# Scans that take their identity from a PSUM bank, and sums of weights spread over three units

## The chip, the cores and the metric

The kernel runs on one core of a Trainium2 chip. The metric is the device time of one execution in microseconds (us), and the median over several executions is compared. The engines are named as in the profile: PE is TensorE, with PEld for its weight loads, DVE is VectorE, ACT is ScalarE, POOL is GpSimd and SP is SyncE, which issues most DMAs.

## The reference, cut to what matters

A state space layer (Mamba2 SSD) over 4 batches, 8 heads, 768 tokens, head size 32 and state size 16 is followed by a two-layer network with a PReLU (256 to 2048 to 256).

```python
cum = np.cumsum(np.log(np.clip(a, 1e-06, 1.0)), axis=-1)       # per chunk
L = np.exp(cum[:, :, :, None] - cum[:, :, None, :]) * causal
M = np.einsum('bhin,bhjn->bhij', Cc, Bc) * L                   # decays times gram matrix
y = M @ xc + (Cc @ state) * np.exp(cum)                        # and the state is carried on
...
h = x @ w_in                                                   # x: 3072 tokens x 256
g = np.maximum(h, 0.0) + alpha * np.minimum(h, 0.0)
out = g @ w_out
```

All data are float32.

## The kernel before, in words

The tokens are cut into chunks of 128, two chunks make a pair (12 pairs), and two pairs make a group of 512 tokens (6 groups). The five engines run the instructions in the order in which the program writes them, one queue for each engine.

**First stage (to about 103 us).** Group 0 goes through the network plainly: `hidden` (L521 to L525) and `output` (L534), in two passes of 256 tokens, while the weights are still being loaded and converted (`convert_a`, `convert`, with POOL at L201 and L230). In between, `ssm` advances the state space layer of pairs 0 to 3.

**Units.** Groups 1 to 5 go through the network in 20 units, `quad(g, z)`: a unit takes four blocks of 128 hidden features (z = 0 to 3) and all 512 tokens, and forms both matrix products by a scheme with 7 block products instead of 8. That scheme needs sums of weights (`weight_sums`, L562, on POOL: `in_sums` from w_in, `out_sums` from w_out, each in four parts for the first (`q0` = 0) and for the last (`q0` = 4) four feature pairs; part 3 overwrites one block of the weights), and sums of tokens (`token_sums`, L574, POOL). In a unit PE fills two PSUM buffers A and Y in turn (L616), ACT and DVE take them out (L624 to L644, and the PReLU at L599 and L601), and POOL forms differences of the results (L650, L659). PE's second products (`product`, L591, n = 1 to 7) of a unit are issued within the unit after it, at the steps of `places`; they accumulate in the four PSUM banks `bank(0)` to `bank(3)`. The fifth product uses the first half of bank 3, and the second half is not used. `combine` (L676 to L698) takes the banks out once per group, within z = 0 of the group after.

**Scans.** `pair` is a generator: each `ssm` call runs it to its next `yield`. For the matrix of decays `dec`, a DVE scan runs over 8 heads x 128 columns: state = a * state + identity, and a zero at the start of each head's row of `a` starts it anew. For pairs 0 and 1 the first operand lies in PSUM (L371), for 2 and 3 one scan of 1024 columns reads both operands from SBUF (L366). For the later pairs 4 to 11 (`fine`), which belong to groups 2 to 5 and are made during the units of groups 1 to 4, `half_decays` (L376) issues scans of 512 columns with `abc` and `ident_h`, both in SBUF. `steps` places them: in z = 0 after steps 2, 3 and 14 and in z = 1 after step 1 for the first pair, in z = 2 after steps 1, 2, 9 and 14 for the second. After the scans come the gram matrices (PE, L475) and their product with the decays (DVE, L480).

`after(j)` is called between the steps of a unit and issues what is due there: products, sums, `combine`, and a stage of a pair, in that order. An instruction that shares a tile with another, in PSUM the tile's bank, waits for it where the program's dependency tracking says so.

Of the kernel before, what the change touches and what calls it, by code (L numbers as in the profile page):

```python
# [12 lines left out]
ALU = mybir.AluOpType  # L13
# [9 lines left out]
def kernel(  # L23
# [25 lines left out]
    nc = tc.nc  # L49
# [7 lines left out]
    Q = 128  # L57
# [16 lines left out]
    HT = GT // 2  # L74
# [25 lines left out]
    def bank(i):  # L100


        return ps_q.tile([P, 512], F32, name="bank", tag=f"q{i}")
# [104 lines left out]
    def convert(dst, src, sg, add=nc.gpsimd):  # L208
# [14 lines left out]
        else:  # L223
            for i in range(2):
# [10 lines left out]
    ident_h = const.tile([P, H * Q], F32, name="ident_h")  # L235
    nc.vector.tensor_copy(out=ident_h.rearrange("p (h t) -> p h t", h=H),
                          in_=ident.unsqueeze(1).to_broadcast([P, H, Q]))
# [40 lines left out]

    held = {}
    bns = {}  # L280

    def rows_scan(i):

        rows = loads.pop(("r", i))
        d0 = prep.tile([RW, Q + 1], F32, name="r0")
        nc.vector.tensor_scalar(out=d0[:, :Q], in0=rows, scalar1=1e-6, scalar2=1.0,
                                op0=ALU.max, op1=ALU.min)
        nc.vector.memset(d0[:, Q:], 0.0)
        pr = prep.tile([RW, Q], F32, name="pr")
        nc.vector.tensor_tensor_scan(out=pr[:, ::-1], data0=d0[:, 1:][:, ::-1],  # L290
                                     data1=ends[:RW, ::-1], initial=0.0,
                                     op0=ALU.mult, op1=ALU.add)
        held[i] = d0
        return pr
# [60 lines left out]
    def pair(gp):  # L355

        b, c = divmod(2 * gp, CPB)
        nat, abc, xt, ap = loads["p", gp]
        last = c + 2 == CPB
        dec = work.tile([P, 2, H, Q], F32, name="dec")  # L360
        dv = dec.rearrange("p k h t -> p k (h t)")
# [10 lines left out]
                                             initial=0.0, op0=ALU.mult, op1=ALU.add)  # L372

        def half_decays(k, w):
            ws = slice(512 * w, 512 * w + 512)
            nc.vector.tensor_tensor_scan(out=dv[:, k, ws], data0=abc[k][:, ws],  # L376
                                         data1=ident_h[:, ws], initial=0.0, op0=ALU.mult,
                                         op1=ALU.add)

        ahead = {}  # L380
        if not abc:
# [7 lines left out]
        if not abc:  # L389
            pf = work.tile([P, 2 * Q], F32, name="pf")  # L390
            nc.vector.tensor_scalar(out=ap, in0=ap, scalar1=1e-6, scalar2=1.0, op0=ALU.max,
                                    op1=ALU.min)
            for k in range(2):
                ks = slice(k * Q, (k + 1) * Q)
                nc.vector.tensor_tensor_scan(out=pf[:, ks], data0=ap[:, ks], data1=zeros,
                                             initial=1.0, op0=ALU.mult, op1=ALU.add)
# [44 lines left out]
        for k in range(nk):  # L441
            for w in range(KC):
                ws = slice(64 * w, 64 * w + 64)
# [21 lines left out]
        if fine:  # L465
            for w in range(2):
                half_decays(1, w)
                yield


        for k in range(2):
# [6 lines left out]
            for r in range(2):  # L478
                hs = slice(4 * r, 4 * r + 4)
# [7 lines left out]
        for k in range(2):  # L487
            if st[k] is not None:
                for w in range(KC):
                    ws = slice(64 * w, 64 * w + 64)  # L490
# [3 lines left out]
        for k in range(2):  # L494
            for w in range(KC):
                for q in range(4):
                    h = 4 * w + q
# [3 lines left out]
        g, q = divmod(2 * gp, GC)  # L501
        if q == 0:
            xts[g] = xtp.tile([P, KC, GT], F32, name="xT")
        for w in range(KC):
            nc.scalar.copy(out=xts[g][:, w, q * Q : (q + 2) * Q],
                           in_=y[w].rearrange("p k t -> p (k t)"))
# [21 lines left out]
    def output(f, half=None):  # L528

        if f == 0:  # L530
            pos[0] = [bank(i).rearrange("p (t m) -> p t m", t=2) for i in range(GC // 2)]
        gt = gts[0, f]
        for t in range(GC) if half is None else range(2 * half, 2 * half + 2):
            nc.tensor.matmul(pos[0][t // 2][:, t % 2], gt[:, t * Q : (t + 1) * Q], w_out[:, f],  # L534
                             start=(f == 0 and t % 2 == 0), stop=(f == NF - 1),
                             skip_group_check=True)
        if f == NF - 1 and half:
            for i, po in enumerate(pos.pop(0)):
                o_sb = op.tile([P, 2, d_model], F32, name="o_sb")
                nc.scalar.copy(out=o_sb, in_=po)  # L540
                t0 = 2 * i * Q
                nc.sync.dma_start(
                    out=out[t0 : t0 + 2 * Q, :].rearrange("(s p) m -> p s m", p=Q), in_=o_sb)
# [5 lines left out]
    wi = w_in.rearrange("p k (q i m) -> p q i k m", i=2, m=P)  # L549
    out_sums, in_sums = [], []  # L550

    def weight_sums(w, sums, q0, part):


        if not sums:
            sums.extend(wld.tile([P, NQ, P], F32, name=f"ws{i}", tag="raw") for i in range(3))
        qs = slice(q0, q0 + 4)
        a11, a12, a21, a22 = w[:, qs, 0, 0], w[:, qs, 0, 1], w[:, qs, 1, 0], w[:, qs, 1, 1]
        s1, s2, s4 = (t[:, qs] for t in sums)
        o, x0, x1, f = ((s1, a21, a22, ALU.add), (s2, s1, a11, ALU.subtract),  # L560
                        (s4, a12, s2, ALU.subtract), (a21, a11, a21, ALU.subtract))[part]
        nc.gpsimd.tensor_tensor(out=o, in0=x0, in1=x1, op=f)  # L562

    wqt = wq.rearrange("p q j i m -> p q i j m")
    xsums = {}

    def token_sums(g):

        b11, b12 = (xts[g][:, 0, h * HT : (h + 1) * HT] for h in range(2))
        b21, b22 = (xts[g][:, 1, h * HT : (h + 1) * HT] for h in range(2))  # L570
        t = xsp.tile([P, 4, HT], F32, name="xs")
        t1, t2, t3, t4 = (t[:, i] for i in range(4))
        for o, x0, x1 in ((t1, b12, b11), (t2, b22, t1), (t3, b22, b12), (t4, b21, t2)):
            nc.gpsimd.tensor_tensor(out=o, in0=x0, in1=x1, op=ALU.subtract)  # L574
        xsums[g] = t1, t2, t3, t4

    ms = {}
# [3 lines left out]
    def product(g, z, n):  # L581

        if z == 0 and n == 1:
            ms[g] = [bank(i).rearrange("p (h t) -> p h t", h=2) for i in range(4)]
        i, h = HALVES[n]
        s1, s2, s4 = out_sums
        for p in range(2):
            q = 2 * z + p
            w = {1: wq[:, q, 0, 0], 2: wq[:, q, 1, 0], 3: s4[:, q], 4: wq[:, q, 1, 1],
                 5: s1[:, q], 6: s2[:, q], 7: wq[:, q, 0, 1]}[n]  # L590
            nc.tensor.matmul(ms[g][i][:, h], w, blocks[g, z][n][:, p],  # L591
                             start=(q == 0 and h == 0), stop=(q == NQ - 1),
                             skip_group_check=True)
# [119 lines left out]
    def finish(g, i):  # L713
        turn(g, i, ends_of[g][i], slice(0, GT), [nc.sync])
# [3 lines left out]
    def ssm(gp, stages=1):  # L718

        if gp not in pairs:  # L720
            pairs[gp] = pair(gp)
        for i in range(stages):
            next(pairs[gp], None)
# [5 lines left out]
    for i in range(3, 6):  # L729
# [9 lines left out]
    first = {1: (1, 1), 4: (1, 1), 6: (1, 1), 8: (1, 1), 10: (1, 1), 12: (1, 1), 14: (2, 1)}  # L739
    second = {0: (2, 1), 1: (2, 1), 2: (2, 1), 3: (2, 1), 5: (2, 1), 6: (3, 1), 7: (3, 1),  # L740
              8: (3, 1), 9: (3, 1), 11: (3, 1), 13: (3, 1)}
    in_steps = {6: ((0, 0), (0, 1)), 8: ((0, 2), (4, 0)), 10: ((4, 1), (4, 2)), 12: ((0, 3),)}
    for n in range(2):
        for f in range(NF):
            i = (n * NF + f) // 2
# [16 lines left out]
            if n and f in in_steps:  # L762
# [2 lines left out]
    early[0] = None  # L765
    token_sums(1)

    steps = {(0, 1): 0, (0, 2): 0, (0, 3): 0, (0, 9): 0, (0, 14): 0,
# [3 lines left out]

    places = {3: 1, 5: 2, 8: 3, 9: 5, 11: 7, 13: 6, 14: 4}
    for i in range(NZ * (NG - 1)):
        g, z = divmod(NZ + i, NZ)
        nxt = 2 * g + 2

        def after(j, g=g, z=z, i=i, nxt=nxt):
            if i and j in places:
                product(*divmod(NZ + i - 1, NZ), places[j])  # L780
            if i == 0:
                if j in (3, 5, 8, 9):
                    output(NF - LAG + (j > 5), {3: 0, 5: 1, 8: 0, 9: 1}[j])
                if j == 2:
                    weight_sums(wi, in_sums, 4, 3)
                if j in (3, 5, 7):
                    weight_sums(wqt, out_sums, 0, {3: 0, 5: 1, 7: 2}[j])
                if j == 10:
                    weight_sums(wqt, out_sums, 0, 3)
            if i == 1 and j in (1, 4, 7, 9):  # L790
                weight_sums(wqt, out_sums, 4, {1: 0, 4: 1, 7: 2, 9: 3}[j])
            if g > 1 and z == 0 and j in (5, 9, 13, 14):
                if j == 5:
                    comb[0] = combine(g - 1)
                next(comb[0], None)
            if g > 1 and z == 1 and j in (10, 13):
                finish(g - 1, j // 13)
            if nxt < NP and (z, j) in steps:
                ssm(nxt + steps[z, j])
            if nxt < NP and (z, j) == (3, 7):  # L800
                token_sums(g + 1)
            ahead = nxt + {(1, 3): 1, (3, 8): 2}.get((z, j), NP)
            if ahead < NP:
                if ahead == 6:
                    rows_turn(1, held["pr"])
                bns[ahead] = pair_loads(ahead)

        comb = [None] if i == 0 else comb
        if z == 0 and nxt < NP:
            if nxt == 4:  # L810
                load_rows(1)
                held["pr"] = rows_scan(1)
                rows_out(1)
            load_pair(nxt + 1)
        if z == 2 and nxt + 2 < NP:
            load_pair(nxt + 2)
        quad(g, z, after)
    for n in (1, 2, 5, 6, 7, 4, 3):
        product(NG - 1, NZ - 1, n)
# [32 lines left out]
```

## Time and profile before

| what | value |
|---|---|
| median of 3 runs | 415.42 us (414.92 to 418.64) |
| the profiled execution | 416.22 us |
| its span in the profile | 414.5 us |
| PE busy | 383.4 us (93%) |
| DVE busy | 274.4 us (66%) |
| POOL busy | 215.8 us (52%) |
| ACT busy | 179.7 us (43%) |
| mean clock granted to PE | 0.983 |

The span runs from the first to the last recorded instruction; the execution is longer by what lies around it. A row of the timeline gives start, duration (us), engine, line, operation, output<-input, shapes and count, and in brackets how long the engine had been idle and what released it. A float32 matmul of one block is recorded as two instructions, and successive ones overlap in the record, so the start of the next instruction tells more than the end of the last.

### The profile page before, as it was taken

How to read it: one execution, taken by the hardware profiler on the slowest of the kernel's cores; microseconds unless marked ns; L12 is line 12 of the kernel's file. 1: busy time of each engine (PE TensorE's matmuls, PEld its weight loads, DVE VectorE, ACT ScalarE, POOL GpSimd, SP SyncE). 2: the span in 40 equal slices, each digit the busy share in tenths (PEclk: the TensorE clock that was granted, in tenths of full speed). 3: DMA queues.
4: the chain of work that ended last, by engine and by line, in shares of the span. 5: the costliest groups of instructions: out<-in, count | busy, mean ns of one | idle time of the engine just before them, and what ended most of it. 6: DMA issues, size and time to landing. Idle time of an engine off the chain costs nothing.

```text
span 414.5 us, 5967 instructions
## 1 busy us (share of the span) xinstructions
PE 383.4 (93%) x2131; PEld 297.4 (72%) x2131; DVE 274.4 (66%) x461; ACT 179.7 (43%) x408; POOL 215.8 (52%) x188
## 2 busy tenths in 40 slices
PE   5778899999889999999999898999998999999993
PEld 4554558778658867777868676868776868888883
DVE  5899894783785674686864775865685864355363
ACT  3464813521444534543444443444443444344540
POOL 3154673689277564472563563553763563464411
PEclk9899969999999999999999999999999999999997
DMA  8939995100583430100691100692100300003003
GB/s 215 228 107 237 299 216 99 56 2 0 75 197 69 93 73 2 51 0 2 102 177 53 52 1 2 95 180 56 51 2 0 53 0 2 1 0 53 0 2 51
DMA packets 124126, 30.58 MB, mean 74 GB/s; under 512 B 96880, under 2 KB 120000, under 8 KB 124096
## 3 DMA queue, kind: packets, MB, share of 16 engines
q1 hardware_dynamic: 117792, 29.67, 31.6%
q10 hardware_dynamic: 6304, 0.52, 1.1%
q8 instruction: 17, 0.28, 0.3%
q14 instruction: 13, 0.11, 0.1%
HBM read 26.85 MB, written 3.34 MB: 73 GB/s over the span
## 4 chain that ended last, share of the span: by engine, by line
PE 73%; DVE 18%; ACT 5%; issue 1%; POOL 1%; DMA 1%; DVEq 0%; ACTq 0%; POOLq 0%
PE hp L616 26%; PE bank L591 25%; DVE dec L376 6%; PE bank L534 5%; PE ss L475 5%; PE hp L521 4%; PE ss L498 2%; DVE dec L371 2%; ACT gt L599 2%; DVE dec L480 1%; DVE wr L227 1%; DVE gt L601 1%; DVE gt L525 1%; PE ss L491 1%; PE ss L444 1%
## 5 line engine op out<-in xcount | busy, mean ns | idle before, releaser
L659 POOL TENSOR_TENSOR gt<-gt 128x512 f32<-128x512 f32 x58 | 90.6, 1563 | 25.3 <-DVE gt L601 11.6
L591 PE MATMUL bank<-gt,w_out 128*128 128x256 f32 x320 | 82.1, 380 | 0.0
L601 DVE SCALAR_TENSOR_TENSOR gt<-hp,s_mul,gt 128x256 f32<-128x256 f32 x120 | 51.9, 478 | 45.3 <-ACT gt L599 41.4
L599 ACT ACTIVATE gt<-hp,s_alpha 128x256 f32<-128x256 f32 x120 | 49.9, 469 | 71.5 <-PE hp L616 70.3
L591 PEld LDWEIGHTS bank<-gt,w_out 128*128 128x128 f32 x320 | 60.3, 190 | 11.3 <-issue 2.3
L650 POOL TENSOR_TENSOR gt<-gt 128x512 f32<-128x512 f32 x20 | 28.7, 1437 | 62.0 <-DVE gt L601 55.7
L591 PE MATMUL bank<-gt,ws 128*128 128x256 f32 x240 | 58.9, 381 | 0.0
L376 DVE TENSOR_TENSOR_SCAN dec<-abc,ident_h 128x512 f32<-128x512 f32 x32 | 55.3, 1759 | 0.0
L591 PEld LDWEIGHTS bank<-gt,ws 128*128 128x128 f32 x240 | 45.2, 190 | 6.7 <-issue 0.8
L616 PE MATMUL hp<-xs,w_in 128*128 128x256 f32 x160 | 43.6, 395 | 1.8 <-ACT u L633 1.4
L616 PE MATMUL hp<-xT,w_in 128*128 128x256 f32 x160 | 41.4, 381 | 1.7 <-DVE gt L601 1.7
L616 PE MATMUL hp<-xs,ws 128*128 128x256 f32 x160 | 42.3, 387 | 0.0
L616 PEld LDWEIGHTS hp<-xs,w_in 128*128 128x128 f32 x160 | 28.1, 189 | 13.1 <-issue 7.4
L616 PEld LDWEIGHTS hp<-xs,ws 128*128 128x128 f32 x160 | 29.1, 190 | 10.1 <-issue 3.7
L616 PEld LDWEIGHTS hp<-xT,w_in 128*128 128x128 f32 x160 | 29.7, 190 | 6.6 <-DVE gt L601 2.9
L601 DVE SCALAR_TENSOR_TENSOR gt<-c,s_mul,gt 128x256 f32<-128x256 f32 x40 | 18.3, 499 | 23.0 <-ACT gt L599 23.0
L480 DVE TENSOR_TENSOR dec<-ss,dec 128x512 f32<-128x512 f32 x40 | 25.7, 682 | 8.7 <-PE ss L475 8.7
L521 PE MATMUL hp<-xT,w_in 128*128 128x256 f32 x96 | 27.6, 412 | 3.8 <-DVE gt L525 3.8
L475 PE MATMUL ss<-cz,bh 64*128 64x512 f32 x80 | 26.2, 660 | 5.0 <-DVE dec L480 3.5
L534 PE MATMUL bank<-w_out,gt 128*128 128x256 f32 x128 | 30.7, 381 | 0.0
L534 PEld LDWEIGHTS bank<-w_out,gt 128*128 128x128 f32 x128 | 24.7, 193 | 3.5
L459 POOL TENSOR_TENSOR sm<-state,bmask 128x256 f32<-128x256 f32 (+1 forms) x12 | 7.7, 638 | 37.2 <-DVE state L455 37.2
(121 smaller groups left out, 537.5 us busy)
## 6 DMA issues: line engine op xcount, KB each, us to landing
abc<-z SPq DMA_DIRECT2D x20, 512.0 KB
raw<-in_moe_w_in_dram SPq DMA_DIRECT2D x8, 512.0 KB
raw<-in_moe_w_out_dram SPq DMA_DIRECT2D x8, 512.0 KB
xt<-in_x_dram SPq DMA_DIRECT2D x24, 128.0 KB
out_dram<-o_sb SPq DMA_DIRECT2D x34, 64.0 KB
nat<-in_B_dram SPq DMA_DIRECT2D x22, 64.0 KB
nat<-in_C_dram SPq DMA_DIRECT2D x22, 64.0 KB
ap<-pf SPq DMA_DIRECT2D x10, 128.0 KB
```

Of the source, the lines that this page charges most:

```text
L371: nc.vector.tensor_tensor_scan(out=dv[:, k, ws], data0=t, data1=ident_h[:, ws], initial=0.0, op0=ALU.mult, op1=ALU.add)
L376: nc.vector.tensor_tensor_scan(out=dv[:, k, ws], data0=abc[k][:, ws], data1=ident_h[:, ws], initial=0.0, op0=ALU.mult, op1=ALU.add)
L475: nc.tensor.matmul(gram[r].rearrange("p h t -> p (h t)"), bh[rs, k], cz[rs, :, k], start=True, stop=True, tile_position=(64 * r, 0), skip_ ...
L480: nc.vector.tensor_tensor(out=dec[:, k, hs], in0=gram[r], in1=dec[:, k, hs], op=ALU.mult)
L521: nc.tensor.matmul(hp, w_in[:, k, f * P : (f + 1) * P], xts[g][:, k, t0 : t0 + nt], start=(k == 0), stop=(k == KC - 1))
L534: nc.tensor.matmul(pos[0][t // 2][:, t % 2], gt[:, t * Q : (t + 1) * Q], w_out[:, f], start=(f == 0 and t % 2 == 0), stop=(f == NF - 1), s ...
L591: nc.tensor.matmul(ms[g][i][:, h], w, blocks[g, z][n][:, p], start=(q == 0 and h == 0), stop=(q == NQ - 1), skip_group_check=True)
L599: nc.scalar.mul(o[:, p], h[:, p], s_alpha[:, fs[p]])
L601: nc.vector.scalar_tensor_tensor(out=o[:, p], in0=h[:, p], scalar=s_mul[:, fs[p]], in1=o[:, p], op0=ALU.mult, op1=ALU.max)
L616: nc.tensor.matmul(to[:, p], w(2 * z + p), b, start=start and p == 0, stop=True, skip_group_check=True)
L650: nc.gpsimd.tensor_tensor(out=tc_, in0=g22, in1=g12, op=ALU.subtract)
L659: eng.tensor_tensor(out=o, in0=x0, in1=x1, op=ALU.subtract)
```

## The change

Three edits. First, the second half of PSUM bank 3 receives 256 columns of the identity (two heads' worth, copied by ACT at the start of the units), and bank 3 is then one tile for all groups, instead of a new tile for each. Second, `half_decays` issues two scans of 256 columns, with that PSUM tile as the second operand, instead of one scan of 512 with `ident_h`: 64 scans in place of 32. Third, the sums of weights are issued at other steps: in the first stage four parts instead of seven, and the other twelve at steps of units 0, 1 and 2 (groups 1, z = 0 to 2) instead of nine in units 0 and 1.

```diff
         def half_decays(k, w):
-            ws = slice(512 * w, 512 * w + 512)
-            nc.vector.tensor_tensor_scan(out=dv[:, k, ws], data0=abc[k][:, ws],
-                                         data1=ident_h[:, ws], initial=0.0, op0=ALU.mult,
-                                         op1=ALU.add)
+            for i in range(2):
+                hs = slice((2 * w + i) * 2 * Q, (2 * w + i + 1) * 2 * Q)
+                nc.vector.tensor_tensor_scan(out=dv[:, k, hs], data0=abc[k][:, hs],
+                                             data1=ident_p[0], initial=0.0, op0=ALU.mult,
+                                             op1=ALU.add)
...
         if z == 0 and n == 1:
-            ms[g] = [bank(i).rearrange("p (h t) -> p h t", h=2) for i in range(4)]
+            ms[g] = [t.rearrange("p (h t) -> p h t", h=2)
+                     for t in [bank(i) for i in range(3)] + m5_bank]
...
-    in_steps = {6: ((0, 0), (0, 1)), 8: ((0, 2), (4, 0)), 10: ((4, 1), (4, 2)), 12: ((0, 3),)}
+    in_steps = {6: ((0, 0),), 8: ((0, 1),), 10: ((0, 2),), 15: ((0, 3),)}
...
+    m5_bank.append(bank(3))
+    ident_p.append(m5_bank[0][:, HT:])
+    nc.scalar.copy(out=ident_p[0], in_=ident_h[:, :HT])
...
+    late_sums = {(0, 2): ((wqt, out_sums, 0, 0),), (0, 4): ((wqt, out_sums, 0, 1),),
+                 (0, 6): ((wqt, out_sums, 0, 2),), (0, 8): ((wi, in_sums, 4, 0),),
+                 (0, 10): ((wqt, out_sums, 0, 3),), (1, 2): ((wi, in_sums, 4, 1),),
+                 (1, 4): ((wi, in_sums, 4, 2),), (1, 8): ((wi, in_sums, 4, 3),),
+                 (2, 2): ((wqt, out_sums, 4, 0),), (2, 4): ((wqt, out_sums, 4, 1),),
+                 (2, 6): ((wqt, out_sums, 4, 2),), (2, 8): ((wqt, out_sums, 4, 3),)}
...
-                if j == 2:
-                    weight_sums(wi, in_sums, 4, 3)
-                if j in (3, 5, 7):
-                    weight_sums(wqt, out_sums, 0, {3: 0, 5: 1, 7: 2}[j])
-                if j == 10:
-                    weight_sums(wqt, out_sums, 0, 3)
-            if i == 1 and j in (1, 4, 7, 9):
-                weight_sums(wqt, out_sums, 4, {1: 0, 4: 1, 7: 2, 9: 3}[j])
+            for w, sums, q0, part in late_sums.get((i, j), ()):
+                weight_sums(w, sums, q0, part)
```

More of the change, by code (lines that the diff above doesn't have):

```diff
@@ L280 @@
     bns = {}
+    ident_p = []
+    m5_bank = []
     def rows_scan(i):
```

## The prediction

> **What bounds the kernel now.** The page first: its busy times and its chain say which engine sets the end and who delays it.
>
> ```profile
> span 414.5 us, 5967 instructions
> PE 383.4 (93%) x2131; PEld 297.4 (72%) x2131; DVE 274.4 (66%) x461; ACT 179.7 (43%) x408; POOL 215.8 (52%) x188
> PE hp L616 26%; PE bank L591 25%; DVE dec L376 6%; PE bank L534 5%; PE ss L475 5%; PE hp L521 4%; PE ss L498 2%; DVE dec L371 2%; ACT gt L599 2%; DVE dec L480 1%; DVE wr L227 1%; DVE gt L601 1%; DVE gt L525 1%; PE ss L491 1%; PE ss L444 1%
> ```
>
> TensorE (PE) bounds it, yet the scans that the change touches (L376) hold 6% of the chain, so at some places PE waits for them. Why they are long is seen in the view of the tile `dec` (count, then min/median/max ns) and in a stretch of the early timeline.
>
> ```profile
> L376 DVE TENSOR_TENSOR_SCAN dec<-abc,ident_h x32: 1199/1978/2287, 107.2 to 337.2; 128x512 f32<-128x512 f32 x32
> L371 DVE TENSOR_TENSOR_SCAN dec<-bank,ident_h x5: 1196/1198/1223, 7.9 to 33.4; 128x512 f32<-128x512 f32 x5
> ...
> 28.62 1.27 POOL L230 TENSOR_TENSOR w_in<-wr,wg 128x512 uint32<-128x512 uint32 x1 [2.90 <-DVE wr L227]
> 29.24 1.21 DVE L371 TENSOR_TENSOR_SCAN dec<-ss,ident_h 128x512 f32<-128x512 f32 x1
> ...
> 180.67 4.76 POOL L659 TENSOR_TENSOR gt<-gt 128x512 f32<-128x512 f32 x3 [0.85 <-DVE gt L601]
> 181.42 0.42 DVE L689 TENSOR_TENSOR c<-u,bank 128x256 f32<-128x256 f32 x1
> ```
>
> The same scan of 512 columns takes 1.20 us at best from SBUF and 1.98 at the median, but never over 1.22 where its first operand lies in PSUM (L371), not even at 29.24, in the middle of a POOL instruction. At 181.42 a VectorE (DVE) sum whose second operand lies in PSUM takes 0.42 us while POOL works from 180.67. So what stretches L376 is that both its operands come from SBUF while POOL reads SBUF; with one in PSUM the trace shows no such stretch.
>
> Now the places where PE waits. First the second group of tokens (from 165 us), timeline, where the bracket names what ended an idle time:
>
> ```profile
> 165.95 4.77 POOL L659 TENSOR_TENSOR gt<-gt 128x512 f32<-128x512 f32 x3 [0.97 <-DVE gt L601]
> ...
> 167.82 3.98 DVE L376 TENSOR_TENSOR_SCAN dec<-abc,ident_h 128x512 f32<-128x512 f32 x2
> ...
> 169.80 0.61 ACT L633 COPY u<-hp 128x512 f32<-128x512 f32 x1
> ...
> 170.56 1.10 PE L616 MATMUL hp<-xs,w_in 128*128 128x256 f32 x4
> ...
> 171.72 0.67 DVE L635 TENSOR_TENSOR hp<-hp,u 128x512 f32<-128x512 f32 x1
> ...
> 172.44 1.13 PE L616 MATMUL hp<-xT,ws 128*128 128x256 f32 x4 [0.78 <-DVE hp L635]
> ...
> 182.09 4.42 DVE L376 TENSOR_TENSOR_SCAN dec<-abc,ident_h 128x512 f32<-128x512 f32 x2
> ...
> 184.95 1.03 PE L591 MATMUL bank<-gt,w_out 128*128 128x256 f32 x4
> ...
> 186.43 1.26 DVE L480 TENSOR_TENSOR dec<-ss,dec 128x512 f32<-128x512 f32 x2
> ...
> 187.14 1.72 PE L475 MATMUL ss<-cz,bh 64*128 64x512 f32 x4 [1.16 <-DVE dec L480]
> ...
> 188.79 1.13 PE L616 MATMUL hp<-xs,w_in 128*128 128x256 f32 x4
> ```
>
> Two stalls a group. **Stall A**: two scans (167.82, for 3.98 us) stand ahead of L635, whose operand from ACT was ready at 169.80 + 0.61 = 170.41; PE waits for L635 until 172.44. **Stall B**: two scans (182.09, for 4.42 us) stand ahead of the products L480, which free the buffer that PE's L475 needs at 187.14. Undisturbed, the same steps run like this in the unit two before (z = 2 and 3):
>
> ```profile
> 150.64 1.03 PE L591 MATMUL bank<-gt,w_out 128*128 128x256 f32 x4
> ...
> 151.60 1.13 PE L475 MATMUL ss<-cz,bh 64*128 64x512 f32 x4
> ...
> 152.66 1.13 PE L616 MATMUL hp<-xs,ws 128*128 128x256 f32 x4
> ...
> 154.49 1.11 PE L616 MATMUL hp<-xs,w_in 128*128 128x256 f32 x4
> 155.43 1.03 PE L616 MATMUL hp<-xT,ws 128*128 128x256 f32 x4
> ```
>
> and the list of waits sums the stalls from 103 us on, over three groups (total, times, longest):
>
> ```profile
> PE ss L475 <- DVE dec L480: 3.5, 3, 1.2
> PE hp L616 <- DVE hp L635: 2.0, 3, 1.1
> ACT cz L413 <- DVE cd L423: 1.2, 1, 1.2
> ```
>
> **The change, part by part. The scans.** Each wide scan becomes two of 256 columns with the identity from PSUM. The trace has no scan of that width. Bounds: 0.37 us (half of the 0.74 below, two scans of 128 columns) and 1.20 (one of 512). On a line between them 256 columns take 0.37 + (1.20 − 0.37)/3 = 0.65 us, which I take: four take 2.6 us, against 2.4 for the undisturbed wide pair and 3.98 to 4.42 at the stalls.
>
> ```profile
> 5.70 0.74 DVE L395 TENSOR_TENSOR_SCAN pf<-ap,zeros 128x128 f32<-128x128 f32 x2
> ```
>
> At one width the trace has 1,196 ns from PSUM (L371) beside 1,199 from SBUF, so no fixed price for PSUM. The Trainium skill, VectorE: DVE Perf Modes, section "The TRN2 errata", speaks against that: its table gives an instruction from PSUM 62 cycles of fixed cost more than one from SBUF, an estimated 0.065 us by its clock. By it the time forecast below would be some 2.3 us longer; the trace decides.
>
> *Stall A*: scans end at 167.82 + 2.6 = 170.42, L635 at about 171.1, and PE's next step is due 155.43 − 154.49 = 0.94 behind 170.56, at 171.50. The stall goes: 172.44 − 171.50 = 0.94, which is the 0.78 of the bracket plus 0.16 of pipeline. For all three: 2.0 + 3 × 0.16 = **2.5**. *Stall B*: scans end at 182.09 + 2.6 = 184.69, both L480 (1.26) at 185.95; L475 is due 151.60 − 150.64 = 0.96 behind 184.95, at 185.91. Gain 1.23, which is 0.07 over the wait of 1.16; for three 3.5 + 0.2 = 3.7. Behind it, L475 to L616 takes 188.79 − 187.14 = 1.65 instead of 152.66 − 151.60 = 1.06: 0.59 × 3 = 1.8. Together **5.5**. The first group has B only in its second form:
>
> ```profile
> 123.15 1.57 PE L475 MATMUL ss<-cz,bh 64*128 64x512 f32 x4
> ```
>
> 1.57 against 1.13: **0.4**. What is late next? Where no scan is in the way PE is itself the limit, and POOL, whose mean of L659 should fall too, has half its time free (columns: PE, PEld, DVE, ACT, POOL busy):
>
> ```profile
> 190.00:228.00 38.00, 38.00 (x239) 30.13 (x238) 23.71 (x41) 18.02 (x42) 17.65 (x15) 1.00 0.49 90
> ```
>
> So the DVE time saved elsewhere is worth nothing; only the stalls are.
>
> **The cost of splitting.** In the third unit of each group a scan runs undisturbed ahead of the activation that PE waits for:
>
> ```profile
> 145.52 1.22 DVE L376 TENSOR_TENSOR_SCAN dec<-abc,ident_h 128x512 f32<-128x512 f32 x1
> ...
> 147.56 0.73 PEld L616 LDWEIGHTS hp<-xT,w_in 128*128 128x128 f32 x4 [0.24 <-DVE gt L601]
> ```
>
> Two of 0.65 are 0.1 more; four groups: **−0.4**. The copy of the identity by ACT comes at the start of the first unit, where ACT waits for PE: nothing, or its length of some 0.4 if that cover were gone.
>
> **The sums of weights** are POOL's, and late ones in the second half of the first stage disturb DVE as well:
>
> ```profile
> 83.38 1.27 POOL L562 TENSOR_TENSOR ws<-ws,w_in 128x512 f32<-128x512 f32 x1
> ...
> 88.46 1.13 PE L521 MATMUL hp<-xT,w_in 128*128 128x256 f32 x4 [0.80 <-DVE gt L525]
> ...
> 103.80 1.27 POOL L562 TENSOR_TENSOR ws<-ws,w_out 128x512 f32<-128x512 f32 x1
> 103.85 1.51 DVE L290 TENSOR_TENSOR_SCAN pr<-r,ends 96x128 f32<-96x128 f32 x1
> ...
> 105.15 1.27 POOL L562 TENSOR_TENSOR ws<-w_out,ws 128x512 f32<-128x512 f32 x1
> 105.28 1.42 DVE L301 TENSOR_TENSOR_SCAN rpf<-r,zeros 96x128 f32<-96x128 f32 x1
> ...
> 109.46 1.10 PE L616 MATMUL hp<-xs,w_in 128*128 128x256 f32 x4 [1.39 <-ACT u L633]
> ```
>
> The sum at 83.38 goes to a later step; POOL's clamp and the DVE steps behind it come about 1.3 us earlier, and PE's 0.80 goes, with 0.16 of pipeline: **0.9** (between 0 and 0.96). At 103.8, scans of 128 columns take 1.51 and 1.42 instead of 0.37 each, beside two sums. Three sums fewer lie ahead of POOL there, and one sum of w_in takes the place of another, so its row could end up to 3 × 1.27 = 3.8 us earlier; but it first has to wait for the tokens' states, so I take half, 1.9: 104.5 instead of 105.15 + 1.27 = 106.4. That spares DVE about one such wait; the stall of 1.39 behind it loses **1.0** (between 0 and 1.39 + 0.16). Moved into the second and third units, the sums meet a POOL half idle: nothing, or 1.27 each where one would delay a block that PE needs.
>
> Sum: 2.5 + 5.5 + 0.4 + 0.9 + 1.0 − 0.4 = 9.9 us. The profiled execution took 416.22 us, of which the span is 414.5; so span 404.6, execution 406.3, and from the median of 415.42 a time of **405.5**.
>
> **The rivals.** *Half of it* (13%): contention goes, but the narrow scans take 0.75 each, or the moved sums bring nothing. With 7 rows of four scans at stalls and 4 pairs in the third units, each 0.1 us more per scan costs 7 × 0.4 + 4 × 0.2 = 3.6; without the sums 1.9 is missing. Time about 409.5. For it: no row shows this scan.
>
> *Slower* (6%): a scan whose second operand is in PSUM is slow or has a fixed cost, at the extreme 1.20 for 256 columns. That is 0.55 over my 0.65: 0.55 × 36 = 19.8 lost against 9.9, time 425. It decides from 9.9/36 = 0.27 more, that is 0.92 us per scan. Against it: L689's 0.42 with the second operand in PSUM.
>
> *A new wait takes its place* (6%): the identity shares its bank with the fifth product of each unit (L591, half 0). The program orders instructions on one PSUM tile even where both only read, as ACT's L413 waited for L423 above, so product 5 will wait for the last scan, and the next scan for product 5. What is behind: on PE's queue every later matmul, on DVE's the activations that free PE's buffers. In the group above the first scans will end at 170.4, and product 5 starts behind the step of 172.44; the scan at 145.52 comes behind a product of the step before. So both waits should be met already. If not, 0.6 us in each of 16 units with scans gives the 9.9 back: 415.4. The Trainium skill, PSUM — Partial Sum Buffer, section "PSUM bank collisions raise a hardware error", demands this order per bank and quadrant even for disjoint columns, so it would not be dropped; no run here shows the error itself.
>
> *Nothing* (5%): POOL and DVE collide over something else than the two operands, a scan's write for instance. Then four narrow scans wait for the same three POOL sums: 416. Against it stands 29.24.
>
> **How the numbers follow.** A measurement of this kernel tells some 1% (4 us) from no change. The forecast holds 70%, its own range 403 to 408. Faster by over 1%: 70 + 13 = 83%. Within 1%: 6 + 5 = 11%. Slower: 6%. The range of 403 to 411 takes in the forecast and the half of it, 83%.
>
> **What would show it.** Right: 64 scans at L376's successor, near 0.65 us with little spread; L659's mean near 1.27 us; no PE wait for L635 or, but for some tenths, L480; PE near 38 of 38 us in the stretches that hold stalls now. The sums: POOL's row ending before 105 us after the first stage, and PE's wait of 1.39 shrunk. Wrong: scans over 0.9 us; a PE wait at L591 or a DVE wait at the scans that names the other; or the stalls gone with PE waiting for ACT at the same places instead.

## The result and the profile after

| | median, us | range, us | ratio to before, 95% interval |
|---|---|---|---|
| before, beside it | 416.00 | 414.92 to 418.64 | |
| after | 404.57 | 404.21 to 404.77 | 0.9715 [0.9667, 0.9763] |
| after, in a second comparison | 404.83 | 403.70 to 405.54 | 0.9728 [0.9681, 0.9774] |

The forecast was 405.5. The profiled execution took 404.59 us against 416.22. The page of the changed kernel, its span, busy times and chain by line (helpers have moved down by 3 or 4 lines: L616 is L620 now, L591 is L595, L376 is L379, L480 is L483, L475 is L478, L635 is L639, L659 is L663):

```profile
span 402.8 us, 6008 instructions
PE 378.4 (94%) x2131; PEld 294.5 (73%) x2131; DVE 255.4 (63%) x493; ACT 180.2 (45%) x409; POOL 192.6 (48%) x188
PE hp L620 30%; PE bank L595 29%; PE bank L537 6%; PE ss L478 5%; PE hp L524 4%; DVE dec L373 2%; PE ss L501 2%; ACT gt L603 1%; DVE wr L227 1%; DVE dec L483 1%; PE ss L407 1%; PE ss L447 1%; DVE gt L528 1%; POOL gt L663 1%; PE ss L494 1%
```

The scans that were changed (L376, now L379), 6% of the chain before, are no longer in the list; L373 is a scan of group 0, which was not changed. DVE and POOL have both become less busy, by 19 and 23 us. Where that comes from is in the view of the tile `dec` (min/median/max ns) and in the groups of both pages; first after, then POOL's group before:

```profile
L379 DVE TENSOR_TENSOR_SCAN dec<-abc,bank x64: 657/661/680, 103.7 to 326.2; 128x256 f32<-128x256 f32 x64
...
L663 POOL TENSOR_TENSOR gt<-gt 128x512 f32<-128x512 f32 x58 | 73.6, 1269 | 29.5 <-DVE gt L605 12.8
```

```profile
L659 POOL TENSOR_TENSOR gt<-gt 128x512 f32<-128x512 f32 x58 | 90.6, 1563 | 25.3 <-DVE gt L601 11.6
```

The spread of the scans is gone, 657 to 680 ns instead of 1,199 to 2,287. POOL's mean fell from 1,563 to 1,269 ns: the contention had cost both sides. PE's waits from 103 us on, the whole list after, where the list of before was headed by 3.5 for L480 and 2.0 for L635:

```profile
PE hp L620 <- DVE gt L605: 1.7, 1, 1.7
PE ss L313 <- ACT xT L508: 1.0, 1, 1.0
```

The second group in the timeline shows both stalls gone, without a bracket at the places where PE waited:

```profile
162.50 3.98 POOL L663 TENSOR_TENSOR gt<-gt 128x512 f32<-128x512 f32 x3 [0.97 <-DVE gt L605]
...
164.38 2.41 DVE L379 TENSOR_TENSOR_SCAN dec<-abc,bank 128x256 f32<-128x256 f32 x4
...
166.36 0.61 ACT L637 COPY u<-hp 128x512 f32<-128x512 f32 x1
...
167.00 0.70 DVE L639 TENSOR_TENSOR hp<-hp,u 128x512 f32<-128x512 f32 x1 [0.22 <-ACT u L637]
...
167.12 1.10 PE L620 MATMUL hp<-xs,w_in 128*128 128x256 f32 x4
...
168.06 1.03 PE L620 MATMUL hp<-xT,ws 128*128 128x256 f32 x4
...
177.59 2.41 DVE L379 TENSOR_TENSOR_SCAN dec<-abc,bank 128x256 f32<-128x256 f32 x4
...
179.92 1.26 DVE L483 TENSOR_TENSOR dec<-ss,dec 128x512 f32<-128x512 f32 x2
...
181.41 1.13 PE L478 MATMUL ss<-cz,bh 64*128 64x512 f32 x4
...
182.47 1.13 PE L620 MATMUL hp<-xs,w_in 128*128 128x256 f32 x4
```

Four scans take 2.41 us, although POOL works through the first 2.10 of them (to 162.50 + 3.98 = 166.48). DVE is now early: at 167.00 it waits 0.22 us for ACT, where ACT's result had to wait for DVE before.

**Where the time came from.** The same PE instruction is looked up in both timelines; the difference between two rows is what was gained up to there.

| PE instruction | before | after | gained so far | gained here |
|---|---|---|---|---|
| first L521 after 60 us | 61.36 | 60.40 | 0.96 | 0.96, not the change |
| the stall of 0.80 in the first stage | 88.46 | 86.64 | 1.82 | 0.86 (sums) |
| the stall of 1.39 in the first unit | 109.46 | 106.36 | 3.10 | 1.28 (sums) |
| stall B in its short form, group 1 | 124.66 | 121.11 | 3.55 | 0.45 |
| group 2: stall A | 172.44 | 168.06 | 4.38 | 0.94 |
| group 2: behind stall B | 188.79 | 182.47 | 6.32 | 1.83 |
| group 3: stall A | 235.48 | 227.97 | 7.51 | 1.23 |
| group 3: behind stall B | 251.61 | 242.16 | 9.45 | 1.83 |
| group 4: stall A | 297.39 | 287.66 | 9.73 | 0.32 |
| group 4: behind stall B | 313.74 | 302.08 | 11.67 | 1.84 |
| last products | 400.39 | 388.76 | 11.63 | −0.04 |

(The small rest, such as −0.11 from group 1 to group 2 and +0.1 between A and B, lies between the rows.) The first 0.96 us is no gain of the kernel. The windows of the first 62 us, in which nothing that the change touches has run yet, have the granted clock behind the five busy times: 0.92 before, 1.00 after, and 0.92 in the second profile of the changed kernel.

```profile
0.00:62.00 62.00, 48.01 (x285) 31.98 (x286) 52.40 (x98) 30.76 (x66) 29.88 (x38) 0.92 0.83 217
```

```profile
0.00:62.00 62.00, 46.98 (x290) 30.82 (x291) 52.44 (x99) 31.56 (x68) 29.88 (x38) 1.00 0.84 217
```

```profile
0.00:62.00 62.00, 47.67 (x285) 31.71 (x286) 52.30 (x98) 30.72 (x66) 29.92 (x38) 0.92 0.85 218
```

The chains of the two profiles of the changed kernel, the first and the second, end accordingly, 1.03 us apart at the last products:

```profile
388.76 7.83 PE bank L595 x36
```

```profile
389.79 7.83 PE bank L595 x36
```

So the change is worth some 10.6 us on the trace (400.39 − 389.79 at equal clock), and 10.8 by the medians of the second comparison (415.63 to 404.83).

### The profile page after: what moved, and what is told of

It is laid out like the page before. It is cut to its first block, busy times and chain, and to the rows that moved or that the text cites. A ratio compares the mean times of both kernels' runs of the same rounds, so it can differ in the third digit from the quotient of the medians.

```text
span 402.8 us, 6008 instructions
## 1 busy us (share of the span) xinstructions
PE 378.4 (94%) x2131; PEld 294.5 (73%) x2131; DVE 255.4 (63%) x493; ACT 180.2 (45%) x409; POOL 192.6 (48%) x188
## 4 chain that ended last, share of the span: by engine, by line
PE 81%; DVE 9%; ACT 3%; POOL 3%; issue 1%; DMA 1%; DVEq 0%; ACTq 0%; POOLq 0%
PE hp L620 30%; PE bank L595 29%; PE bank L537 6%; PE ss L478 5%; PE hp L524 4%; DVE dec L373 2%; PE ss L501 2%; ACT gt L603 1%; DVE wr L227 1%; DVE dec L483 1%; PE ss L407 1%; PE ss L447 1%; DVE gt L528 1%; POOL gt L663 1%; PE ss L494 1%
## 5 line engine op out<-in xcount | busy, mean ns | idle before, releaser
L663 POOL TENSOR_TENSOR gt<-gt 128x512 f32<-128x512 f32 x58 | 73.6, 1269 | 29.5 <-DVE gt L605 12.8
L595 PE MATMUL bank<-gt,w_out 128*128 128x256 f32 x320 | 82.1, 380 | 0.0
L605 DVE SCALAR_TENSOR_TENSOR gt<-hp,s_mul,gt 128x256 f32<-128x256 f32 x120 | 51.8, 477 | 44.8 <-ACT gt L603 41.7
L603 ACT ACTIVATE gt<-hp,s_alpha 128x256 f32<-128x256 f32 x120 | 50.0, 469 | 62.6 <-PE hp L620 61.3
L595 PEld LDWEIGHTS bank<-gt,w_out 128*128 128x128 f32 x320 | 60.3, 190 | 11.3 <-issue 2.3
L595 PE MATMUL bank<-gt,ws 128*128 128x256 f32 x240 | 58.9, 381 | 0.0
L654 POOL TENSOR_TENSOR gt<-gt 128x512 f32<-128x512 f32 x20 | 25.4, 1270 | 64.4 <-DVE gt L605 64.4
L595 PEld LDWEIGHTS bank<-gt,ws 128*128 128x128 f32 x240 | 45.2, 190 | 6.7 <-issue 0.8
L620 PE MATMUL hp<-xs,w_in 128*128 128x256 f32 x160 | 43.6, 395 | 0.5
L620 PE MATMUL hp<-xT,w_in 128*128 128x256 f32 x160 | 41.5, 382 | 1.7 <-DVE gt L605 1.7
L620 PE MATMUL hp<-xs,ws 128*128 128x256 f32 x160 | 42.3, 387 | 0.0
L379 DVE TENSOR_TENSOR_SCAN dec<-abc,bank 128x256 f32<-128x256 f32 x64 | 39.0, 665 | 0.0
L620 PEld LDWEIGHTS hp<-xs,w_in 128*128 128x128 f32 x160 | 28.1, 189 | 11.9 <-issue 5.9
L620 PEld LDWEIGHTS hp<-xs,ws 128*128 128x128 f32 x160 | 29.1, 190 | 10.1 <-issue 3.7
L620 PEld LDWEIGHTS hp<-xT,w_in 128*128 128x128 f32 x160 | 29.7, 190 | 6.7 <-DVE gt L605 3.1
L483 DVE TENSOR_TENSOR dec<-ss,dec 128x512 f32<-128x512 f32 x40 | 25.6, 682 | 10.5 <-PE ss L478 10.5
L605 DVE SCALAR_TENSOR_TENSOR gt<-c,s_mul,gt 128x256 f32<-128x256 f32 x40 | 17.7, 483 | 23.0 <-ACT gt L603 23.0
L524 PE MATMUL hp<-xT,w_in 128*128 128x256 f32 x96 | 25.7, 390 | 4.4 <-DVE gt L528 4.4
L639 DVE TENSOR_TENSOR hp<-hp,u 128x512 f32<-128x512 f32 x20 | 14.0, 700 | 21.7 <-ACT u L637 21.4
```

The costliest lines, as they stand in the source:

```text
L379: nc.vector.tensor_tensor_scan(out=dv[:, k, hs], data0=abc[k][:, hs], data1=ident_p[0], initial=0.0, op0=ALU.mult, op1=ALU.add)
L483: nc.vector.tensor_tensor(out=dec[:, k, hs], in0=gram[r], in1=dec[:, k, hs], op=ALU.mult)
L524: nc.tensor.matmul(hp, w_in[:, k, f * P : (f + 1) * P], xts[g][:, k, t0 : t0 + nt], start=(k == 0), stop=(k == KC - 1))
L595: nc.tensor.matmul(ms[g][i][:, h], w, blocks[g, z][n][:, p], start=(q == 0 and h == 0), stop=(q == NQ - 1), skip_group_check=True)
L603: nc.scalar.mul(o[:, p], h[:, p], s_alpha[:, fs[p]])
L605: nc.vector.scalar_tensor_tensor(out=o[:, p], in0=h[:, p], scalar=s_mul[:, fs[p]], in1=o[:, p], op0=ALU.mult, op1=ALU.max)
```

## The experiments

Theory: the scan has two SBUF operands and fights POOL for SBUF; with one operand in PSUM it doesn't. Rivals: the narrower instructions do it alone; the scans' write collides; the sums of weights bring most of it; a new wait at bank 3 eats part of it.

**Narrow scans, identity still in SBUF.** Same count, same width, only the memory of the second operand differs from the changed kernel.

```diff
-                                             data1=ident_p[0], ...
+                                             data1=ident_h[:, hs], ...
```

> As the changed kernel, but the 64 narrow scans read the identity from SBUF again. Theory (two SBUF operands collide with POOL): each narrow scan waits for the POOL instruction in progress, and four of them alternate with three POOL sums of 1.27 us, so a row takes about 3 x (1.27 + 0.65) = 5.8 us at most, 4.5 at least, instead of 2.4; the stalls of before come back and are 0.3 to 1.2 us longer at 7 places: 416 to 421 us. Rival 1 (it is the narrowness, finer turns between DVE and POOL, that helped): 404.5 to 407. Rival 2 (the moved sums brought the gain): about 405.

Measured 437.16 us (431.82 to 437.46), ratio 1.053 [1.0512, 1.0547]: slower than before, far beyond the 416 to 421 expected. Tile `dec`, two rows of its timeline, and the waits of PE:

```profile
L379 DVE TENSOR_TENSOR_SCAN dec<-abc,ident_h x64: 658/1450/1739, 103.4 to 353.4; 128x256 f32<-128x256 f32 x64
```

```profile
184.03 5.49 DVE L379 TENSOR_TENSOR_SCAN dec<-abc,ident_h 128x256 f32<-128x256 f32 x4
...
190.15 1.72 PE L478 MATMUL ss<-cz,bh 64*128 64x512 f32 x4 [2.24 <-DVE dec L483]
```

```profile
PE ss L478 <- DVE dec L483: 8.6, 4, 2.2
PE hp L620 <- DVE hp L639: 6.4, 7, 1.5
PE hp L620 <- DVE gt L605: 5.2, 5, 1.7
```

At best a scan takes the same from either memory, 658 and 657 ns, so PSUM itself is neither faster nor slower; at the median it takes 1,450 ns from SBUF and 661 from PSUM. That settles one side of the mechanism: it is the second SBUF operand. The write, the same in both, is not it. That POOL is the other side, its trace shows as well: the 12 scans during which POOL runs nothing take 658 to 681 ns, and every longer one, up to 1,739, overlaps a POOL instruction. After, 60 of the 64 scans overlap POOL, and none takes over 680. One row of four has both kinds: two scans of 1.30 and 1.69 us beside POOL, then two of 0.66 when POOL is done (167.79 + 4.23 = 172.02):

```profile
167.79 4.23 POOL L663 TENSOR_TENSOR gt<-gt 128x512 f32<-128x512 f32 x3 [0.98 <-DVE gt L605]
...
169.66 4.07 DVE L379 TENSOR_TENSOR_SCAN dec<-abc,ident_h 128x256 f32<-128x256 f32 x4
```

The Trainium skill, SBUF — State Buffer, section "Who interferes with whom", says that a DVE instruction with two SBUF inputs contends with a GpSimd instruction that reads SBUF, and one with a single SBUF input, outside the modes in which DVE uses two ports, does not; these two traces agree, 1,450 against 661 ns.

Narrowness alone harms: the kernel with the sums alone, further down, has the same sums and the wide scans from SBUF and takes 415.18 us against 437.16 here. My expectation had the row right (5.49 us, within 4.5 to 5.8) and the stalls wrong: it let the 7 known ones grow by 0.3 to 1.2 us each, but L639 alone now makes PE wait 7 times and not 3, and L605 5 times and not once. The best reading is that every separate instruction can lose a turn to POOL, so twice as many lose more turns; what one loses at most is the same at both widths, 2,287 − 1,199 = 1,088 ns for the wide scans of before and 1,739 − 658 = 1,081 ns for the narrow ones. The timed runs of this kernel are some 5 us longer than its profiled one of 431.82, with a mean granted clock of 0.970 to 0.978 against 0.986; what makes the difference stays open.

**The scans alone, and the sums alone.** The first takes the new scans with the old places of the sums, the second the reverse.

```diff
-    in_steps = {6: ((0, 0),), 8: ((0, 1),), 10: ((0, 2),), 15: ((0, 3),)}
+    in_steps = {6: ((0, 0), (0, 1)), 8: ((0, 2), (4, 0)), 10: ((4, 1), (4, 2)), 12: ((0, 3),)}
...            # late_sums out, the old steps of the sums in
```

> Scans as changed, sums of weights at the steps of before. Theory: the scans bring about 8.0 of the gain, the sums 2 (0.9 at the stall before 90 us, 1.0 to 1.3 at the one before 110 us): about 406.7 us, 2 above the changed kernel. Rival 2 (sums): about 413. Rival 3 (neither alone, they need each other): 411 or more.

Measured 407.41 us (406.36 to 408.32), ratio 0.9809 [0.9788, 0.983], 0.7 us above the 406.7 expected. Its timeline keeps the stall at the first unit that the sums caused:

```profile
110.05 1.10 PE L620 MATMUL hp<-xs,w_in 128*128 128x256 f32 x4 [1.41 <-ACT u L637]
```

```diff
-            for i in range(2):
-                hs = ...; tensor_tensor_scan(..., data1=ident_p[0], ...)
+            ws = slice(512 * w, 512 * w + 512)
+            tensor_tensor_scan(..., data1=ident_h[:, ws], ...)
...            # and bank 3 is a new tile for each group again, without the identity
```

> Sums at the steps of the changed kernel, scans wide and from SBUF as before. Theory: 2 us faster than before, about 413.5, with the stalls behind L376 still there (PE waiting 3.5 us for the products and 2.0 for the sum behind the scans). Rival 2: about 406. Rival 3: as before, 415 or more.

Measured 415.18 us (414.17 to 417.23), ratio 0.9995 [0.9977, 1.0013]: nothing, where 2 us was expected. The timeline shows the gain come and go. At 115.34 PE is 2.04 us ahead of before; at 146.43 (147.56 before) only 1.13 is left:

```profile
142.51 1.28 POOL L564 TENSOR_TENSOR w_out<-w_out 128x512 f32<-128x512 f32 x1
...
142.74 1.73 DVE L603 SCALAR_TENSOR_TENSOR gt<-c,s_mul,gt 128x256 f32<-128x256 f32 x2 [1.15 <-ACT gt L601]
...
146.43 1.13 PE L618 MATMUL hp<-xT,w_in 128*128 128x256 f32 x4 [0.69 <-DVE gt L603]
```

A sum that was moved to the third unit runs beside a DVE instruction (L603 here, L605 after) that also reads two operands from SBUF, c and gt. Two of these take 1.73 us instead of 0.88, and PE waits 0.69. In the changed kernel the sum and L605 miss each other: POOL, no longer held up by the scans (three of its differences just before take 3.96 us there and 5.56 here), is done with the sum before DVE begins (139.39 + 1.29 = 140.68):

```profile
139.39 1.29 POOL L565 TENSOR_TENSOR w_out<-w_out 128x512 f32<-128x512 f32 x1
...
141.23 0.88 DVE L605 SCALAR_TENSOR_TENSOR gt<-c,s_mul,gt 128x256 f32<-128x256 f32 x2 [1.15 <-ACT gt L603]
```

So the two parts of the change don't quite add up. By the medians the sums bring 407.41 − 404.57 = 2.8 us beside the new scans and at most about 1 beside the old ones. Part of the 2.8 is not theirs: in the profile of the scans alone the first L524 after 60 us, ahead of all that was changed, starts at 61.91, against 61.36 before and 60.40 after. Counted from that instruction to the last products, the sums bring 2.2 us beside the new scans and 1.2 beside the old ones. The difference of 1.0 us is smaller than what the intervals of the timed runs can tell. The kernel with the sums alone was repeated with more runs, together with one that moves the colliding sum.

> sums_only once more, with more rounds. Its profile had PE 2.0 us ahead of before in the first unit and then a new wait of 0.69 us in the third (DVE's activation L603 of 1.73 us beside a moved sum), leaving 1.1. If that is the whole: 0.5 to 1.3 us faster than before. If the moved sums bring nothing without the new scans: 0.3 or less.

Measured 414.64 us (413.63 to 415.39), ratio 0.9966 [0.9945, 0.9987]: 1.0 us, near the 1.1 us by which its first profile ended earlier (399.28 against 400.39 at the last products).

```diff
-                 (2, 6): ((wqt, out_sums, 4, 2),), (2, 8): ((wqt, out_sums, 4, 3),)}
+                 (2, 6): ((wqt, out_sums, 4, 3),), (2, 12): ((wqt, out_sums, 4, 2),)}
```

> sums_only with the last moved sum of the third unit taken out of DVE's way: part 3 at step 6, part 2 at step 12. If the collision of that sum with L603 (both its operands in SBUF) ate the gain: the new wait of 0.69 goes, 1.5 to 2.1 us faster than before. If it was something else: as sums_only2.

Measured 414.70 us (412.41 to 416.00), ratio 0.9972 [0.9949, 0.9995]. The timeline shows the collision gone and PE 2.24 ahead of before at this place:

```profile
142.48 0.89 DVE L603 SCALAR_TENSOR_TENSOR gt<-c,s_mul,gt 128x256 f32<-128x256 f32 x2 [1.15 <-ACT gt L601]
...
145.32 1.13 PE L618 MATMUL hp<-xT,w_in 128*128 128x256 f32 x4
```

Yet the time isn't told apart from the kernel without the swap, and the profiled execution ended only 0.56 earlier than before at the last products (399.83). Its page has a dip of the granted clock in the 25th slice of 40, which neither the page of before nor that of the unswapped kernel has there:

```profile
PEclk9999969999999999999999998999999999999998
```

From 248.50 to 258.80 us the clock is 0.83. Just ahead of that, at stall B of group 3, PE is still 2.24 us ahead of before (247.72 against 249.96); from there to the L618 that follows L500 (256.36) takes 8.64 us, against 6.96 in the kernel without the swap (248.84 to 255.80), so 1.68 us go in the dip. In this profile the removed wait was therefore kept up to the dip; that it was worth time in the timed runs is not shown.

**Twice as many scans again.** 128 scans of 128 columns, to price an extra instruction.

```diff
-            for i in range(2):
-                hs = slice((2 * w + i) * 2 * Q, (2 * w + i + 1) * 2 * Q)
+            for i in range(4):
+                hs = slice((4 * w + i) * Q, (4 * w + i + 1) * Q)
...
-                                             data1=ident_p[0], ...
+                                             data1=ident_p[0][:, :Q], ...
```

> As the changed kernel, but each scan is cut again, 128 scans of 128 columns with the identity from PSUM. Theory: a row of eight takes 8 x 0.37 = 3.0 us instead of 2.4, with no collisions; stall A has some 0.3 us of slack and takes the rest, stall B has none (0.6 at four places), the pairs in the third units cost 0.25 at four: 3 to 4.5 us more, 408 to 409. Rival 4 (scans are now wholly off the path): 404.6. If the price of one more instruction is larger than the line through 128 and 512 columns says: above 410.

Measured 405.00 us (404.60 to 405.71), ratio 0.9754 [0.9739, 0.9769]: as fast as the change, 3 to 4 us below what was expected. Tile and timeline:

```profile
L379 DVE TENSOR_TENSOR_SCAN dec<-abc,bank x128: 391/394/416, 103.5 to 326.8; 128x128 f32<-128x128 f32 x128
```

```profile
164.28 2.59 DVE L379 TENSOR_TENSOR_SCAN dec<-abc,bank 128x128 f32<-128x128 f32 x8
```

Eight take 2.59 us in a row, four of double width 2.41: an extra instruction costs (2.59 − 2.41)/4 = 0.045 us. In a row of eight that is 0.32 us an instruction, less than the 0.39 recorded for one, so successive scans overlap in the record. I had multiplied recorded lengths.

**Scans replaced by something trivial.** Each pair of scans becomes one fill of 512 columns; the decays of pairs 4 to 11 are not computed.

```diff
-            for i in range(2): ...scan...
+            ws = slice(512 * w, 512 * w + 512)
+            nc.vector.memset(dv[:, k, ws], 0.5)
```

> The 64 scans are left out: a fill of 512 columns with a constant stands in their places, so the decays of pairs 4 to 11 are not computed. Theory (the scans no longer set the end anywhere): what is left of their cost is some 0.3 us at three places and 0.1 at others, so 403.5 to 404.6, within 1 us of the changed kernel. Rival 4 (narrow scans still cost something on the path): 402.5 or less. Rival 5 (the fill reads nothing, so POOL runs freer and other waits shrink as well): below 403 with POOL's sums shorter than 1.27 us.

Measured 404.47 us (404.33 to 404.79), ratio 0.9722 [0.968, 0.9765]; the changed kernel beside it took 404.83. With 32 fills of 0.485 us instead of 64 scans of 0.66, and without any scan that reads bank 3, the timed runs gain nothing clear of their scatter. Counted from the first L521 after 60 us to the last products, the profile is 0.4 us shorter than that of the changed kernel. So what the scans cost beyond such fills, together with any wait between them and the products in bank 3, is about 0.4 us.

**The stall that is left.** The list of waits after has 1.7 us at L605, in the first unit. There ACT takes out an output of group 0 (L543) ahead of the PReLU (L603). And the 1.0 at L313 is a transposition on PE that waits for ACT in the fourth unit, with PE's other products queued behind it. Two kernels put that output three steps later; the second also moves the call with the transposition from step 8 to step 11 of z = 3.

```diff
-                if j in (3, 5, 8, 9):
-                    output(NF - LAG + (j > 5), {3: 0, 5: 1, 8: 0, 9: 1}[j])
+                if j in (3, 5, 8, 12):
+                    output(NF - LAG + (j > 5), {3: 0, 5: 1, 8: 0, 12: 1}[j])
...            # second kernel only:
-            ahead = nxt + {(1, 3): 1, (3, 8): 2}.get((z, j), NP)
+            ahead = nxt + {(1, 3): 1, (3, 11): 2}.get((z, j), NP)
```

> The changed kernel, with the last half block of the first group's output issued three steps later in the first unit, so that ACT's two copies of 0.57 us come behind the activations that PE's 1.72 us wait hangs on. If that wait is as the profile says: 402.5 to 403.2. If the copies then delay the first products of the second unit, or g11's activations: 404 or more.

Measured 404.10 us (403.50 to 404.85), ratio 0.9714 [0.9661, 0.9766]: 0.7 below the changed kernel beside it, less than expected and within the scatter; the profiles, counted as above, give 0.6. After and here, the stall shrank from 1.72 to 0.79:

```profile
114.28 1.13 PE L620 MATMUL hp<-xT,w_in 128*128 128x256 f32 x4 [1.72 <-DVE gt L605]
```

```profile
113.80 1.13 PE L620 MATMUL hp<-xT,w_in 128*128 128x256 f32 x4 [0.79 <-DVE gt L605]
```

The output in front of L603 was the cause of 0.93 of the wait; I had put down the whole of it. What holds the other 0.79 was not looked into further.

> As out_late, and the transposes of the second set of rows (PE waits 1.0 us there for ACT) moved behind the next matmuls in that unit: another 1.0 to 1.3 us less, 401.3 to 402.2. If POOL's product behind them then comes too late for the next pair's state: as out_late or slower.

Measured 402.54 us (402.27 to 402.84), ratio 0.9675 [0.9633, 0.9717]: the best version, 2.3 us under the changed kernel of the same comparison, whose runs (403.70 to 405.54) it doesn't overlap. It is 1.6 us below the kernel with the output alone, where 1.0 to 1.3 was expected, and still above the 401.3 to 402.2 expected in all, because the first step had brought less. The profiles, counted as above, put it 1.8 us ahead of the changed kernel. Its L313 no longer waits; first the row of the kernel with the output alone, then that of this one, and its whole list of PE's waits from 100 us on:

```profile
156.25 0.30 PE L313 MATMUL ss<-ident,pr 96*128 96x96 f32 x1 [1.00 <-ACT xT L508]
```

```profile
157.66 0.25 PE L313 MATMUL ss<-ident,pr 96*128 96x96 f32 x1
```

```profile
PE hp L620 <- DVE gt L605: 0.8, 1, 0.8
```

## Why the prediction was right

**The mechanism** held: contention over two SBUF operands, ended by moving one. It was argued from L371 and L689 and is now shown by a pair of kernels that differ only in the memory of one operand, and by the scans that met POOL and those that did not. No rival came about. In particular no PE instruction waits at L595 for DVE, the scans have no idle time before them, and replacing the scans by fills gains about 0.4 us on the trace.

**Stall A**: 2.5 predicted, 0.94 + 1.23 + 0.32 = 2.49 measured. **Stall B** with the step behind it: 5.5 predicted, 1.83 + 1.83 + 1.84 = 5.50. **Group 1**: 0.4 and 0.45. Both stalls ended as the working put them, PE at its own pace: in the second group (busy PE is the first figure behind the window's length) the stretch with both stalls had 21.43 of 23.50 us before and has 20.88 of 21.00 after.

```profile
165.50:189.00 23.50, 21.43 (x98) 15.83 (x97) 18.26 (x27) 9.78 (x23) 14.05 (x11) 1.00 0.07 22
```

```profile
162.00:183.00 21.00, 20.88 (x100) 15.95 (x99) 14.77 (x30) 9.79 (x23) 11.56 (x11) 1.00 0.09 26
```

**Sums.** The first stall gave 0.86 (0.9 predicted). The second gave 1.28 (1.0 predicted): this term was undersized. POOL's row ended about where I had put it: at 101.20 + 1.27 = 102.47, which is 104.3 on the time scale of before, as PE is 1.82 us ahead by then, against my 104.5. One of the two scans of 128 columns still meets it and the other is free, so one such wait is spared, 1.42 − 0.39 = 1.03 us, as priced. What I left out is the DVE instruction just ahead of these scans, L286 (now L288), which became 1.28 − 0.61 = 0.67 us shorter. First before, then after:

```profile
102.46 1.27 POOL L562 TENSOR_TENSOR ws<-w_out 128x512 f32<-128x512 f32 x1
102.53 1.28 DVE L286 TENSOR_SCALAR r<-rows 96x128 f32<-96x128 f32 x1
```

```profile
99.96 1.27 POOL L565 TENSOR_TENSOR ws<-w_out,ws 128x512 f32<-128x512 f32 x1
...
100.70 0.61 DVE L288 TENSOR_SCALAR r<-rows 96x128 f32<-96x128 f32 x1
...
101.20 1.27 POOL L565 TENSOR_TENSOR ws<-w_in 128x512 f32<-128x512 f32 x1
...
101.36 1.39 DVE L292 TENSOR_TENSOR_SCAN pr<-r,ends 96x128 f32<-96x128 f32 x1
...
102.67 0.39 DVE L303 TENSOR_TENSOR_SCAN rpf<-r,zeros 96x128 f32<-96x128 f32 x1
```

The whole stall of 1.39 went. L286 is also a warning not to read the rule too widely: it has one tensor operand in SBUF and still waits for POOL. Both times it ends 0.08 us behind the sum of POOL that it meets (103.81 behind 103.73, 101.31 behind 101.23), and with POOL idle, at 4.72 us, it takes 0.22.

That the moved sums cost nothing in the second and third units held, but, as the kernel with the sums alone shows, only since the new scans let POOL run early. The step was right for a reason that I hadn't named.

**Splitting**: −0.4 predicted, −0.04 to −0.11 a group and −0.23 in all measured. The scan of 256 columns was put at 0.65 and is 0.66, but a row of four takes 2.41, not 2.6. The line through 128 and 512 columns hit the length of one instruction; that lengths can be summed was the mistake, and it also spoilt the expectation for 128 columns.

Sum: 9.9 predicted, 10.6 at equal clock; the difference is these two terms and 0.3 us between stalls A and B that no step had.

## What to carry to other kernels

When a DVE instruction has a wide spread of durations, compare the same operation with its operands in other memories and look at what POOL does at that moment; a constant operand moved to an unused half bank of PSUM takes DVE and POOL apart without making either faster by itself. Shortening the instructions without moving the operand made it worse here. And price work by the waits of the bounding engine: 16 us of DVE time in the scans was worth 8 us, at seven places, and replacing the scans that are left by shorter fills about 0.4 us.

## What the runs showed of the hardware that was not expected

- Splitting a contended instruction in two about doubled what the contention costs: 32 scans had 55.3 us, 16.9 more than 32 of the shortest (1.199), and 64 with the same operands 76.4 us, 34.3 more than 64 of the shortest (0.658); 64 with the identity in PSUM had 39.0 us. The kernel with the sums alone has 55.4 us for its 32 scans, so the places of the sums do not matter to this (the groups on the pages of before, of the narrow kernel in SBUF and of after, with the busy time and the mean in ns behind the first bar):

```profile
L376 DVE TENSOR_TENSOR_SCAN dec<-abc,ident_h 128x512 f32<-128x512 f32 x32 | 55.3, 1759 | 0.0
```

```profile
L379 DVE TENSOR_TENSOR_SCAN dec<-abc,ident_h 128x256 f32<-128x256 f32 x64 | 76.4, 1247 | 0.0
```

```profile
L379 DVE TENSOR_TENSOR_SCAN dec<-abc,bank 128x256 f32<-128x256 f32 x64 | 39.0, 665 | 0.0
```

- Successive scans overlap in the record: eight of 0.39 us each end 2.59 us after the first begins.
- In some executions the granted clock falls to 0.92 over the first 62 us, in the same program, and about 1 us is lost there, as much as several of the effects above. In the twelve profiles the first matmul of L521 (or its successor) after 60 us on the chain starts at 61.20 to 61.91 where that clock is 0.92 or 0.94, and at 60.15 to 60.56 where it is 0.97 or 1.00. What decides it is open.
